# GpSimd in place of VectorE for the lower parts of the first eight weight halves

## The chip, the cores and the metric

The kernel runs on one core of a Trainium2 chip. The metric is device time in microseconds (us), the median of the runs of one launch. Engines are called by the profile's names: PE (TensorE; PEld is its weight load), DVE (VectorE), ACT (ScalarE), POOL (GpSimd), SP (SyncE, which issues transfers here).

## The reference

An attention with a decaying state, a feed-forward layer, and a mixture of eight experts whose weights are balanced by eight rounds of row and column sums:

```python
for t in range(S):                                   # r, k, v, w: (2, 8, 768, 48)
    cur = einsum('bhd,bhe->bhde', u * k_t, v_t)
    y[:, :, t] = einsum('bhd,bhde->bhe', r_t, state + cur)
    state = w_t[..., None] * state + einsum('bhd,bhe->bhde', k_t, v_t)
x = y as (1536, 384)
h = x @ w_in                                         # (384, 2048), float64
x = (h * clip(h + 3, 0, 6) / 6) @ w_out              # (2048, 384), float64
P = exp(x @ w_gate - max); 8 x (rows to 1, columns to N / E)
out = sum over e of P[:, e:e+1] * (max(x @ w1[e], 0) @ w2[e])    # E = 8, F = 1024
```

## The kernel before, in words

Every matmul is made of three in a 32-bit form (`float32r`): each operand is split into an upper part (`hi`, the value rounded to `float32r`) and a lower part (`lo = x - hi`), and the products hi·hi, hi·lo and lo·hi are added in PSUM.

The work has three stages. (1) Attention in 12 steps (six blocks of 128 tokens by two batches), and, woven into it, the feed-forward layer in 96 units. A unit takes 128 of the 2048 hidden columns for 256 tokens: nine matmuls up (`ph`, line 407), ACT adds 3 and clips (`t`, L412), DVE multiplies (L415), ACT takes the upper part `gh` (L419), DVE the lower part `gl` (L423), and nine matmuls down (`xa` and `xb`, L440). (2) From about 298 us on, the eight experts, 24 units each, with 128x512 tiles. (3) The last tiles and their stores.

The feed-forward weights come as float64. They are loaded as 32-bit words in 16 halves, two for each of eight column groups `i`: half `i0` of `w_in` (`n` = 0, tiles `wah` and `wal`) and half `i1` of `w_out` (`n` = 1, tiles `wbh` and `wbl`), 128x768 words after the conversion. `half_steps` gives the steps of one half, which `fast` names by a letter and the two digits:

- `W` (`middle`, L125), `Q` (`top`, L129), `q` (`bottom`, L133): three DVE operations put the float32 bits together in the tile `x`;
- `h` (`upper`, L195): ACT writes the upper part;
- `l` (`lower`, L200): `lo = x - hi`, with both inputs in SBUF.

So `l20` is the lower part of half 0 of group 2. The order of the halves is 00, 01, 10, 11, 20, 21, 30, 31 and so on. The tile `x` has two buffers (`tmp`, `"x"`), so `W` of a half waits until `l` of the half two before it has read its buffer. Expert weights are float32 and need only `h` and `l` (steps `sa` to `se`, later `split_chunk`).

The order of stage 1 is a list of step names, `ORDER`, written out by hand. Each engine takes its instructions in that order, so a step that waits holds up all that stands behind it on its engine. Other steps that the text names, with the chunk's two digits or the unit's number behind: `Z`, `z` (POOL, L280 and L284, 128x384 products) and `D` (DVE, L288, their sums); `N`, `n` (POOL, L320, masks on the attention tile `a`); `Y` (PE, L333 and L337, attention outputs), `y` (DVE, L349, `ys`), `X` (PE, L368, transposes), `H` (ACT, L374, `x1h`), `L` (DVE, L378, `x1l`); `u` (DVE, L358, two updates of the state `st`), `s` (ACT, L363, its decay); `p` and `d` (PE, up and down), `t` (ACT, L412), `g` (DVE, L415), `gh`, `gl` (ACT L419, DVE L423), `oa`, `ob` (the sums of a group of units). `_` is a small matmul that only fills time on PE.

```python
        def lower():
            self.lower_part("ab"[n], q["x"].bitcast(F32), q["hi"], key, eng)
...
    def lower_part(self, nm, x, hi, key, eng):
        lo = self.wp.tile([128, KT * CH], F32R, tag=f"w{nm}l", name=f"w{nm}l")
        eng.tensor_tensor(out=lo, in0=x, in1=hi.bitcast(F32), op=ALU.subtract)
...
    J30 O30 q11 y20 w30 h11 p.4 u20 M21 l11 T21 s20 N21 X20 D21 d.2 t.4 W21 i30 H20 g.4 V21 d.3 L20 Q20 gh.4 p.5 m21
```

The last line is one of the lines of `ORDER`.

Of the kernel before, what the change touches and what calls it, by code (L numbers as in the profile page):

```python
# [94 lines left out]
class Kernel:  # L95
# [803 lines left out]
    def fast(self):  # L899
        tc, nc, pool = self.tc, self.nc, self.pool  # L900
        self.general = False
        with ExitStack() as top:
# [65 lines left out]
            for i in range(F1 // CH):  # L968
                for n in range(2):
                    steps[f"w{i}{n}"] = lambda i=i, n=n: self.load_half(i, n)  # L970
                    for s, fn in zip("WQqhl", self.half_steps(i, n, nc.vector)):
                        steps[f"{s}{i}{n}"] = fn
            for i in range(NCH):
                steps[f"load{i}"] = lambda i=i: self.load_chunk(i)
# [19 lines left out]
            for e in range(1, E):  # L994
                for i in range(NCH):
                    n = (e - 1) * 24 + 4 * i + 6
# [106 lines left out]
```

## Time and profile before

| | before |
|---|---|
| median of 3 runs | 1106.01 us (1104.5 to 1106.65) |
| profiled execution | 1106.59 us, span of its trace 1104.8 us |
| PE busy | 1089.0 us (99%), 6021 matmuls |
| DVE busy | 620.9 us (56%), 1220 instructions |
| ACT busy | 329.7 us (30%), 690 |
| POOL busy | 47.5 us (4%), 54 |
| granted PE clock, mean | 0.990 |

The profile page cuts the span into 40 slices of 27.6 us. Its DVE line begins 8999996: DVE is at 80 to 90% and more of its time through the first six slices (165 us) and near half after that, so the average of 56% hides a first stage in which it has hardly any idle time. A busy PE is not PE at its peak: the granted clock (1.0 is 2.4 GHz, 0.50 is 1.2 GHz) says at what rate it ran. In the timeline, an instruction's start and length are given, and in brackets how long its engine was idle before it and which work ended that.

### The profile page before, as it was taken

What the parts mean: (1) busy time and instruction counts of PE and PEld (TensorE: products, weight loads), DVE (VectorE), ACT (ScalarE), POOL (GpSimd) and SP (SyncE); (2) the same over time, 40 slices, a digit from 0 to 9 for tenths busy, and PEclk for the clock granted to TensorE, in tenths of its full rate; (3) what the DMA queues carried; (4) which work ended last, traced back from release to release, by engine and by line L of the source; (5) the groups of instructions that cost most, each with busy time, mean ns of one, the idle gap of its engine ahead of it and who ended that gap; (6) DMA issues with size and microseconds to landing.
All of it is one profiled execution on the core that took longest, in us unless ns stands there. A gap on an engine that the chain in (4) does not pass through costs nothing.

```text
span 1104.8 us, 14961 instructions
## 1 busy us (share of the span) xinstructions
PE 1089.0 (99%) x6021; PEld 942.9 (85%) x6021; DVE 620.9 (56%) x1220; ACT 329.7 (30%) x690; POOL 47.5 (4%) x54
## 2 busy tenths in 40 slices
PE   9999999999999999999999999999999999999997
PEld 7889999999978888888888888888888888788887
DVE  8999996444533534554564555565466756433231
ACT  4565565544522321221221221122112212221211
POOL 2330042000000000000000000000000000000000
PEclk8899999999999999999999999999999999999999
DMA  8564234000110005013201220313233242100001
GB/s 269 148 184 140 93 102 149 2 1 1 58 58 30 1 6 176 1 42 111 83 26 54 95 78 26 111 56 100 87 114 114 84 144 87 58 1 30 29 15 46
DMA packets 45741, 83.14 MB, mean 75 GB/s; under 512 B 3840, under 2 KB 27744, under 8 KB 45664
## 3 DMA queue, kind: packets, MB, share of 16 engines
q1 hardware_dynamic: 45520, 82.01, 23.3%
q8 instruction: 49, 0.80, 0.3%
q14 instruction: 28, 0.23, 0.1%
q10 hardware_dynamic: 144, 0.10, 0.0%
HBM read 79.69 MB, written 2.41 MB: 74 GB/s over the span
## 4 chain that ended last, share of the span: by engine, by line
PE 91%; DVE 6%; DMA 1%; issue 1%; ACT 1%; SPq 0%; POOL 0%; DVEq 0%; POOLq 0%
PE ph L576 36%; PE y L610 34%; PE ph L407 7%; PE xa L440 5%; PE xb L440 2%; PE y L608 2%; PE y L337 1%; DVE x L133 1%; DVE gl L423 1%; PE sc L304 1%; DVE x L129 1%; DVE t L415 1%; DMA rk<-in_dm_dram 1%; DVE e L238 1%; PE y L333 1%
## 5 line engine op out<-in xcount | busy, mean ns | idle before, releaser
L585 DVE SCALAR_TENSOR_TENSOR hl<-ph,hh 128x512 fp32r<-128x512 f32 x192 | 132.4, 690 | 377.8 <-ACT hh L581 376.7
L581 ACT ACTIVATE hh<-ph 128x512 fp32r<-128x512 f32 x192 | 114.9, 598 | 610.9 <-PE ph L576 610.9
L576 PE MATMUL ph<-x2h,wah 128*128 128x512 f32 x576 | 226.1, 393 | 0.9 <-DVE off L748 0.9
L576 PE MATMUL ph<-x2h,wal 128*128 128x512 f32 x576 | 224.4, 390 | 0.0
L576 PE MATMUL ph<-x2l,wah 128*128 128x512 f32 x576 | 224.2, 389 | 0.0
L610 PE MATMUL y<-hl,wbh 128*128 128x512 f32 x552 | 214.8, 389 | 0.0
L610 PE MATMUL y<-hh,wbh 128*128 128x512 f32 x552 | 214.8, 389 | 0.0
L610 PE MATMUL y<-hh,wbl 128*128 128x512 f32 x552 | 214.7, 389 | 0.0
L576 PEld LDWEIGHTS ph<-x2h,wah 128*128 128x128 f32 x576 | 108.1, 188 | 23.1 <-DVE off L748 1.0
L576 PEld LDWEIGHTS ph<-x2h,wal 128*128 128x128 f32 x576 | 108.1, 188 | 22.9
L576 PEld LDWEIGHTS ph<-x2l,wah 128*128 128x128 f32 x576 | 108.2, 188 | 21.8
L610 PEld LDWEIGHTS y<-hh,wbl 128*128 128x128 f32 x552 | 103.6, 188 | 21.6
L610 PEld LDWEIGHTS y<-hl,wbh 128*128 128x128 f32 x552 | 103.6, 188 | 21.6
L610 PEld LDWEIGHTS y<-hh,wbh 128*128 128x128 f32 x552 | 103.6, 188 | 21.5
L407 PE MATMUL ph<-x1h,wah 128*128 128x256 f32 x288 | 82.6, 287 | 1.0 <-ACT wah L195 1.0
L407 PE MATMUL ph<-x1h,wal 128*128 128x256 f32 x288 | 81.4, 282 | 0.3 <-DVE wal L200 0.3
L407 PE MATMUL ph<-x1l,wah 128*128 128x256 f32 x288 | 81.2, 282 | 0.0
L415 DVE SCALAR_TENSOR_TENSOR t<-t,ph 128x256 f32<-128x256 f32 x96 | 40.0, 418 | 37.1 <-ACT t L412 36.8
L412 ACT ACTIVATE t<-ph,three 128x256 f32<-128x256 f32 x96 | 45.2, 471 | 52.3 <-PE ph L407 51.6
L407 PEld LDWEIGHTS ph<-x1h,wah 128*128 128x128 f32 x288 | 54.7, 190 | 1.9 <-ACT wah L195 1.2
L440 PE MATMUL xa<-gh,wbh 128*128 128x256 f32 x192 | 55.4, 288 | 0.6 <-DVE x2f L452 0.6
L407 PEld LDWEIGHTS ph<-x1h,wal 128*128 128x128 f32 x288 | 54.9, 190 | 0.6 <-DVE wal L200 0.6
(147 smaller groups left out, 1393.2 us busy)
## 6 DMA issues: line engine op xcount, KB each, us to landing
stg<-in_w_dram SPq DMA_DIRECT2D x64, 384.0 KB, 5.1
stg<-in_w_in_dram SPq DMA_DIRECT2D x8, 768.0 KB, 4.9
stg<-in_w_out_dram SPq DMA_DIRECT2D x8, 768.0 KB, 4.4
pb<-pd SPq DMA_DIRECT2D x8, 768.0 KB, 4.2
seen<-in_w_in_dram SPq DMA_DIRECT2D x8, 768.0 KB, 4.9
seen<-in_w_out_dram SPq DMA_DIRECT2D x8, 768.0 KB, 4.4
rk<-in_dm_dram SPq DMA_DIRECT2D x12, 448.0 KB, 4.3
seen<-in_dm_dram SPq DMA_DIRECT2D x12, 448.0 KB, 3.7
```

The costliest lines, as they stand in the source:

```text
L129: nc.vector.scalar_tensor_tensor(out=q["x"], in0=q["high"], scalar=0xC0000000, in1=q["x"], op0=ALU.bitwise_and, op1=ALU.bitwise_or)
L133: nc.vector.scalar_tensor_tensor(out=q["x"], in0=q["low"], scalar=29, in1=q["x"], op0=ALU.logical_shift_right, op1=ALU.bitwise_or)
L238: nc.vector.tensor_tensor_scan(out=e.rearrange("p i t -> p (i t)"), data0=w[:, :WCOL - 1], data1=self.d1e.rearrange("p i t -> p (i t)"), i ...
L407: nc.tensor.matmul(ph, wa[:, kt, :], xa[:, kt, :], start=n == 0, stop=n == 3 * KT - 1)
L412: nc.scalar.activation(q["t"], q["ph"], AF.Relu, bias=self.three)
L415: nc.vector.scalar_tensor_tensor(out=q["t"], in0=q["t"], scalar=6.0, in1=q["ph"], op0=ALU.min, op1=ALU.mult)
L440: nc.tensor.matmul(o, wb[:, kt * 128:(kt + 1) * 128], ga, start=start and n == 0 and kt != 1, stop=stop and n == 2, skip_group_check=True)
L576: nc.tensor.matmul(ph, wa[:, kt, :], xa[:, kt, sl], start=n == 0, stop=n == 3 * KT - 1)
L581: nc.scalar.activation(q["hh"], q["ph"], AF.Relu)
L585: nc.vector.scalar_tensor_tensor(out=hl, in0=q["ph"], scalar=0.0, in1=q["hh"].bitcast(F32), op0=ALU.max, op1=ALU.subtract)
L608: nc.tensor.matmul(y[:, :DM], ha[:, sl], wb, **go)
L610: nc.tensor.matmul(y, wb[:, sl], ha, **go)
```

## The change

In `fast`, the engine handed to the lower part of a half is GpSimd for the groups 0 to 3 (eight halves) and VectorE for the other eight:

```diff
@@ -968,7 +968,7 @@
             for i in range(F1 // CH):
                 for n in range(2):
                     steps[f"w{i}{n}"] = lambda i=i, n=n: self.load_half(i, n)
-                    for s, fn in zip("WQqhl", self.half_steps(i, n, nc.vector)):
+                    for s, fn in zip("WQqhl", self.half_steps(i, n, nc.gpsimd if i < 4 else nc.vector)):
                         steps[f"{s}{i}{n}"] = fn
```

`ORDER` is as it was. The instruction order of PE, ACT and SP is the same; eight instructions leave DVE's list and enter POOL's.

POOL, from the attention of the third chunk on (`wbl` is step `l11`, then `l20`, `l21`, `l30`, `l31`; `rkt` are the steps `Z` and `z`, `a` the masks):

```order
 L280 TENSOR_TENSOR rkt<-rkt 128x384
 L284 TENSOR_TENSOR rkt<-rkt,ubt 128x384
+L200 TENSOR_TENSOR wbl<-x,wbh 128x768
 L320 AFFINE_SELECT a<-a 128x512 x2
 L280 TENSOR_TENSOR rkt<-rkt 128x384
 L284 TENSOR_TENSOR rkt<-rkt,ubt 128x384
+L200 TENSOR_TENSOR wal<-x,wah 128x768
+L200 TENSOR_TENSOR wbl<-x,wbh 128x768
+L200 TENSOR_TENSOR wal<-x,wah 128x768
+L200 TENSOR_TENSOR wbl<-x,wbh 128x768
 L280 TENSOR_TENSOR rkt<-rkt 128x384
```

`l11` now stands ahead of two masks, and `l20` behind the two products of the next chunk.

DVE, around step `l11` (`st_94` is the state update `u20`, the reduction is `D21`, the last row is `W21`):

```order
 L349 TENSOR_TENSOR ys<-y,dv 128x384
 L358 TENSOR_TENSOR st_94<-u,st_94 48x4x48 x2
-L200 TENSOR_TENSOR wbl<-x,wbh 128x768
 L288 TENSOR_REDUCE sd<-rkt 128x8
 L125 TENSOR_SCALAR x<-stg 128x768
```

`W21` needs the buffer that `l11` reads, and `l11` is on another engine now.

DVE, around steps `l20` and `l21` (`ys` is `y21`, `st_95` is `u21`, `x1l` is `L21`, the last row is `W30` and `W31`):

```order
 L349 TENSOR_TENSOR ys<-y,dv 128x384
 L358 TENSOR_TENSOR st_95<-u,st_95 48x4x48 x2
-L200 TENSOR_TENSOR wal<-x,wah 128x768
-L200 TENSOR_TENSOR wbl<-x,wbh 128x768
 L378 TENSOR_TENSOR x1l<-xp,x1h 128x3x128
 L125 TENSOR_SCALAR x<-stg 128x768 x2
```

Two instructions leave the place between the state update `u21` and `L21`. `l30` leaves the place behind the pair `gl.8` and `gl.9`, and `l31` that behind `W40`.

## Rows read from the trace of the kernel before

**Rows 1.** Busy time by engine in three stretches: PE, PEld, DVE, ACT, POOL, PE clock.
```profile
60.00:100.00 40.00, 38.43 (x321) 36.74 (x321) 39.05 (x69) 24.38 (x58) 6.86 (x5) 1.00 0.58 181
100.00:130.00 30.00, 30.00 (x253) 29.70 (x253) 28.70 (x52) 15.30 (x33) 2.36 (x2) 1.00 0.29 95
130.00:165.00 35.00, 33.21 (x311) 31.64 (x309) 34.56 (x63) 21.70 (x63) 11.10 (x12) 1.00 0.32 99
```

**Rows 2.** The chain that ended last, pieces before 100 us: start, us, what.
```profile
36.85 2.01 PE sc L304 x16
...
50.55 6.17 DMA rk<-in_dm_dram
...
82.88 0.86 PE xa L440 x5
```

**Rows 3.** Line 200 on DVE, lower parts of w_out halves: ns min/median/max, first and last start.
```profile
L200 DVE TENSOR_TENSOR wbl<-x,wbh x8: 927/952/959, 37.4 to 140.4; 128x768 fp32r<-128x768 f32 x8
```

**Rows 4.** Timeline of POOL: start, us, what, idle before.
```profile
1.08 0.29 POOL L768 TENSOR_SCALAR_AFFINE_SELECT ident<-ones 128x128 f32<-128x128 f32 x1
...
20.68 1.00 POOL L284 TENSOR_TENSOR rkt<-rkt,ubt 128x384 f32<-128x384 f32 x1
...
44.22 0.64 POOL L320 TENSOR_SCALAR_AFFINE_SELECT a<-a 128x512 f32<-128x512 f32 x1 [3.12 <-ACT a L318]
44.83 1.01 POOL L280 TENSOR_TENSOR rkt<-rkt 128x384 f32<-128x384 f32 x1
...
59.04 3.08 POOL L284 TENSOR_TENSOR rkt<-rkt,ubt 128x384 f32<-128x384 f32 x1
```

**Rows 5.** Timeline of DVE beside two of those POOL products.
```profile
20.71 0.56 DVE L349 TENSOR_TENSOR ys<-y,dv 128x384 f32<-128x384 f32 x1 [1.99 <-PE y L337]
21.18 1.30 DVE L200 TENSOR_TENSOR wal<-x,wah 128x768 fp32r<-128x768 f32 x1
...
44.93 1.18 DVE L423 TENSOR_TENSOR gl<-t,gh 128x256 fp32r<-128x256 f32 x1 [0.34 <-ACT gh L419]
```

**Rows 6.** Timeline of PE where group 1 is first used.
```profile
50.98 0.46 PE L407 MATMUL ph<-x1h,wah 128*128 128x256 f32 x1 [1.03 <-ACT wah L195]
...
51.98 0.58 PE L407 MATMUL ph<-x1h,wal 128*128 128x256 f32 x1 [0.32 <-DVE wal L200]
```

**Rows 7.** Timeline of ACT: steps h11, h20, s21, H21, h30.
```profile
62.97 0.84 ACT L195 ACTIVATE wbh<-x 128x768 fp32r<-128x768 f32 x1 [4.39 <-DVE x L133]
...
70.75 0.83 ACT L195 ACTIVATE wah<-x 128x768 fp32r<-128x768 f32 x1
...
74.93 1.17 ACT L363 ACTIVATE st<-st,pt 112x96 f32<-112x96 f32 x4 [0.66 <-DVE st L358]
76.01 0.47 ACT L374 ACTIVATE x1h<-xp 128x384 fp32r<-128x384 f32 x1
...
80.66 0.84 ACT L195 ACTIVATE wah<-x 128x768 fp32r<-128x768 f32 x1
```

**Rows 8.** Timeline of DVE: steps W21, q21, u21, L21, ob.7, gl.8 with gl.9, W41.
```profile
65.40 0.55 DVE L125 TENSOR_SCALAR x<-stg 128x768 uint32<-128x768 uint32 x1
...
72.45 0.95 DVE L133 SCALAR_TENSOR_TENSOR x<-stg,x 128x768 uint32<-128x768 uint32 x1
...
74.13 0.71 DVE L358 TENSOR_TENSOR st<-u,st 48x192 f32<-48x192 f32 x2
...
76.73 0.56 DVE L378 TENSOR_TENSOR x1l<-xp,x1h 128x384 fp32r<-128x384 f32 x1
...
82.07 0.42 DVE L448 TENSOR_SCALAR x2f<-xb 128x256 f32<-128x256 f32 x1
82.41 0.75 DVE L423 TENSOR_TENSOR gl<-t,gh 128x256 fp32r<-128x256 f32 x2
...
87.34 0.55 DVE L125 TENSOR_SCALAR x<-stg 128x768 uint32<-128x768 uint32 x1
```

**Rows 9.** Busy time and clock in the ten microseconds of group 6.
```profile
50.00:60.00 10.00, 8.70 (x63) 8.41 (x64) 9.36 (x18) 7.04 (x21) 3.56 (x4) 0.83 0.68 207
```

## The prediction

> **What bounds the kernel now.** I read the busy times by stretch first. From 60 to 100 us DVE is busy for 39.05 of 40 us and PE stands idle for 1.57; from 100 to 130 us PE has no idle time; from 130 to 165 us it is idle for 1.79 again [rows 1]. The reader is to see two things: PE is the bound of the whole, DVE is nearly level with it before 165 us, and a microsecond that PE loses before 100 us can't be made up, since PE is full behind it. In the other direction there is little to win: all PE idle time in the DVE-bound stretch is 1.57 us.
>
> Next the chain that ended last. Before 45 us it runs over PE (scores at 36.85), at 50.55 over a 6.17 us transfer of `rk`, from there over DVE, and at 82.88 it goes to PE for good, behind `gl.8` [rows 2]. So lateness of DVE between 56 and 83 us counts, and what happens to DVE before 50 us is covered by PE and that transfer.
>
> Last the timelines, for what a GpSimd product does to its neighbours [rows 4, 5]. This is the main point.
>
> **The price of a lower part on GpSimd.** On DVE it takes 0.95 us [rows 3]. No 128x768 operation on POOL is in the trace. From below I bound it by DVE's 0.95, from above by twice a 128x384 product, 2 x 1.01 = 2.0. A select takes 0.29 for 128 columns and 0.64 for 512, which leaves 0.17 fixed; (1.01 - 0.17) x 2 + 0.17 = 1.85 us, which I take [rows 4].
>
> The GPSIMD Engine Reference of the Trainium skill (section 3.1) gives 4497 ns for a two-input operation of 2048 columns; an estimate from that page for 768 columns is 1.69 us, and with it each of the three waits below would be 0.16 shorter, the sum 2.1 in place of 2.55. The row differs, 1.01 for 384 columns where that rate gives an estimate of 0.84, so the row decides.
>
> **What it does to DVE meanwhile.** Two `gl` take 0.75 together at 82.41 and one takes 1.18 at 44.93; the difference of 0.8 lies beside the POOL product at 44.83. At 20.68 another product starts: `ys`, which reads PSUM and one SBUF tile, takes 0.56, and the lower part behind it 1.30 in place of 0.95, since the product is not over before 21.68 [rows 3 to 5, 8]. So a DVE operation with two SBUF inputs waits for most of a POOL product, some 0.8 of 1.01 us, and one with a PSUM input doesn't. For a lower part I take 1.65 of its 1.85 us (bounds: 0 and 2.0).
>
> SBUF — State Buffer of the Trainium skill (section Who interferes with whom) says that such a DVE operation and a GpSimd operation that reads SBUF exclude each other for the whole instruction, and that the one issued first blocks the other. The traced blocks are a little shorter than the whole; by that page's rule two terms below would each be 0.2 larger, and the sum 2.95.
>
> **The change, term by term,** in times of the old trace.
>
> `l00`, `l01`, `l10`: 0. The first two lie where PE leads [rows 2]. `l10` comes 1 us later to PE, which waited 0.32 for it at 51.98 [rows 6]; DVE then waits for the `rk` transfer, which was issued behind `q10`, ahead of `l10`. If that cover is gone, the price is 1.0.
>
> `l11`: `W21` needs the buffer of `x` that `l11` reads. `h11` ends at 62.97 + 0.84 = 63.81, GpSimd needs 1.85 more, with 0.1 for two handovers 65.8; `W21` was at 65.40 [rows 7, 8]. **+0.4.** From below: 0.95 gives 64.9, no loss. From above: the mask queued behind `l11` on POOL holds `W21` for another 0.5. The 0.95 us that left DVE win nothing, since `W21` is next but one.
>
> `l20`: `h20` ends at 71.58; ACT is 0.4 to 0.5 late there, the products ahead on POOL are done, and GpSimd begins near 72.1 and blocks until 73.8. `q21`, two SBUF inputs, was due at 72.45 + 0.4 = 72.85 [rows 7, 8]. **+1.0** (0 to 1.3).
>
> The gap of `l20` and `l21`: `L21` needs `x1h`, and so `u21`, then `s21` and `H21` on ACT. Before, `u21` ended at 74.84 and `L21` began at 76.73, 1.89 later; the two lower parts filled that gap. Without them it is 0.09 to start ACT, 1.08 and 0.47 of work and a handover, 1.7: **-0.2** and not the 1.7 us that left DVE [rows 7, 8]. `l21` runs on GpSimd meanwhile and blocks nobody.
>
> `l30`: `h30` (80.66 to 81.5) is 1.2 late by now, so `l30` is ready at 82.7. `Q31`, two inputs from SBUF, keeps it out until `ob.7`, one from PSUM, which began at 82.07 and is due at 83.3; there GpSimd gets in and holds until 84.95. `gl.8` was due at 82.41 + 1.2 = 83.6 [rows 7, 8]. **+1.35** (0 to 1.6). PE waits for `gl.8` at 82.88 [rows 2], so the lateness passes to PE here.
>
> `l31`: `W41`, before at 87.34, waits for it as `W21` did for `l11` [rows 8]; but PE, itself 2.5 late by then, feeds the DVE rows around it, and that lateness covers the wait. 0.
>
> Sum: 0.4 + 1.0 - 0.2 + 1.35 = **2.55 us** (bounds -0.2 and 3.8, from the ends named). Behind 100 us nothing gives it back [rows 1]. The weight loads that the `q` steps release go later by no more than this, and the order of SP is unchanged. The profiled execution took 1106.59, 0.58 above the median; against the median, 1106.01 + 2.55, some **1108.6 us**.
>
> **The rivals.**
>
> *No blocking.* GpSimd takes 1.85 us but DVE runs on. For it: the DVE operations with a PSUM input do so, and a POOL product took 3.08 at 59.04, so POOL can also be the one that waits [rows 4, 5]. Against it: 0.8 us lost where a product met a two-input operation. Then only the waits stay: `W21` +0.4, the gap -0.2, `gl.8` +0.2, and 1106.2 us. It decides if `q21` and `gl.8` keep their lengths and starts. This is the case that ends on the other side, no slower than before.
>
> *PE falls to the lower clock.* PE stood for 1.03 us at 50.98, and behind it a matmul takes 0.46 and 0.58; the mean granted clock of these 10 us is 0.83, so it was at 0.50 (1.2 GHz) for 3.4 of them [rows 6, 9]. The forecast has new waits of a microsecond or more: at 51.98, before the transposes that need `y21`, and before `gl.8`. That spell cost 1.7 us of work. One or two between 73 and 90 us add 1.5 to 3: 1110.1 to 1111.6. Against it: from 60 to 100 us PE stood for 1.57 in all and the clock stayed at 1.00 [rows 1].
>
> *DVE gains.* The lower parts end on GpSimd before anyone needs them and DVE gets the room. Its most is PE's idle time: 1.57 us, 1104.4; only with the stretch behind 130 us as well, 3.36 in all, 1102.7 [rows 1]. It needs a lower part on GpSimd near 1 us.
>
> **How the numbers follow.** About 0.2%, 2.2 us, can be told from no change here. Forecast 0.60: its sum lies near that bound, 0.43 of it above and 0.17 below. No blocking 0.22, all within. Lower clock 0.12, all slower. DVE gains 0.06, of which 0.05 faster, 0.01 within. So faster 0.05, same 0.40, slower 0.55. The range begins at 1105.0, no blocking with an execution's scatter, and ends at 1111.8, the dear end of the lower clock; left out are most of the gains and the tails, under 0.2.
>
> **What would show it.** Eight rows of line 200 on POOL with a shortest length near 1.85. `q21` starting about a microsecond behind its neighbour `g.6`, or drawn out to 1.9; `gl.8` drawn out by over a microsecond; `W21` with an idle time ahead of it that ends with POOL; `L21` as late behind `u21` as before, with DVE idle between. PE's wait before `gl.8` longer, PE from 100 to 130 us still without idle time, and the clock at 1.00 from 60 us on. It is wrong if `gl.8` starts within 0.5 us of 82.41, if POOL's rows of line 200 are near 1 us, or if the difference arises behind 100 us.

## The result and the profile after

| | before | changed |
|---|---|---|
| median of 6 runs each, us | 1104.61 (1103.28 to 1106.65) | 1110.92 (1108.73 to 1113.14) |
| ratio, 95% interval | 1 | 1.0061 [1.0046, 1.0075] |
| profiled execution, its span, us | 1106.59, 1104.8 | 1113.14, 1111.4 |

The change makes the kernel slower by 6.7 us (5.1 to 8.3) by the ratio; the medians lie 6.3 apart. The direction and the range of the prediction held. The size did not: the sum gave 2.55 us. Part of the closeness of 1108.6 to 1110.92 is luck, since before came out 1.4 us lower in six runs than in the first three. That the range held is luck of the same kind: seen from 1106.01, the median it was built on, it reached from -1.0 to +5.8 us, and the measured loss lies above that.

The profiled execution of the changed kernel is the slowest of its six. It is already 1.3 us late when PE starts on group 1 (`52.28`, before 50.98 [rows 6]). That much is scatter between executions or an effect of the early pieces; the experiments come back to it.

First the page of the changed kernel: the span, and busy time, share and instructions of each engine.

```profile
span 1111.4 us, 14960 instructions
...
PE 1089.3 (98%) x6021; PEld 943.2 (85%) x6021; DVE 617.3 (56%) x1212; ACT 330.0 (30%) x690; POOL 61.4 (6%) x62
```

Next line 200 in it, grouped by engine: ns min/median/max, first and last start; below that, who waited for these instructions (us, times).

```profile
L200 POOL TENSOR_TENSOR wal<-x,wah x4: 1810/1999/2519, 21.1 to 86.9; 128x768 fp32r<-128x768 f32 x4
L200 POOL TENSOR_TENSOR wbl<-x,wbh x4: 1822/1842/1997, 39.4 to 92.2; 128x768 fp32r<-128x768 f32 x4
...
  DVE x L125: 2.7, 3
```

Eight products run on POOL, the shortest in 1.81 us (forecast 1.85, on DVE 0.95 [rows 3]). Three times the next step `W` on DVE stands behind one of them.

Then the stretches of the changed kernel, columns as in [rows 1].

```profile
60.00:100.00 40.00, 35.41 (x289) 34.21 (x288) 33.28 (x57) 21.83 (x54) 15.37 (x10) 0.96 0.48 148
100.00:130.00 30.00, 30.00 (x256) 29.89 (x255) 28.55 (x51) 15.20 (x33) 2.24 (x2) 1.00 0.43 138
...
70.00:80.00 10.00, 7.59 (x63) 7.39 (x62) 8.76 (x12) 5.53 (x16) 7.46 (x5) 0.94 0.69 227
80.00:90.00 10.00, 8.63 (x63) 8.26 (x63) 7.94 (x14) 4.56 (x11) 2.18 (x1) 0.89 0.29 92
```

From 60 to 100 us DVE falls from 39.05 to 33.28 us busy, with 57 instructions in place of 69: some went to POOL, others now come later than 100 us. Yet PE's idle time there grows from 1.57 to 4.59. From 100 to 130 us PE has no idle time, as before: nothing is given back. New is the granted clock: 0.94 and 0.89 in the two stretches where it was 1.00 before.

The timeline of DVE in the changed kernel shows the steps of [rows 8]: `W21`, `q21`, `gl.6`, `u21`, `L21`, `gl.8` with `gl.9`, `W41` (start, us, what, idle before and what ended it).

```profile
66.97 0.97 DVE L125 TENSOR_SCALAR x<-stg 128x768 uint32<-128x768 uint32 x1 [1.13 <-POOL wbl L200]
...
74.30 1.42 DVE L133 SCALAR_TENSOR_TENSOR x<-stg,x 128x768 uint32<-128x768 uint32 x1
75.64 2.03 DVE L423 TENSOR_TENSOR gl<-t,gh 128x256 fp32r<-128x256 f32 x1
...
78.06 0.71 DVE L358 TENSOR_TENSOR st<-u,st 48x192 f32<-48x192 f32 x2
80.45 0.56 DVE L378 TENSOR_TENSOR x1l<-xp,x1h 128x384 fp32r<-128x384 f32 x1 [1.67 <-ACT x1h L374]
...
87.66 2.04 DVE L423 TENSOR_TENSOR gl<-t,gh 128x256 fp32r<-128x256 f32 x2
...
94.08 0.56 DVE L125 TENSOR_SCALAR x<-stg 128x768 uint32<-128x768 uint32 x1 [0.32 <-POOL wbl L200]
```

And POOL beside them in the same execution: `l11`, `l20`, `l21`, `l30`.

```profile
65.11 1.82 POOL L200 TENSOR_TENSOR wbl<-x,wbh 128x768 fp32r<-128x768 f32 x1 [4.24 <-ACT wbh L195]
...
74.87 2.52 POOL L200 TENSOR_TENSOR wal<-x,wah 128x768 fp32r<-128x768 f32 x1
77.35 2.00 POOL L200 TENSOR_TENSOR wbl<-x,wbh 128x768 fp32r<-128x768 f32 x1
86.89 2.18 POOL L200 TENSOR_TENSOR wal<-x,wah 128x768 fp32r<-128x768 f32 x1 [7.55 <-ACT wah L195]
```

For `gl.6` and for PE's first step behind `y21`, these are the rows of the kernel before:

```profile
73.32 0.41 DVE L423 TENSOR_TENSOR gl<-t,gh 128x256 fp32r<-128x256 f32 x1
...
74.26 0.55 PE L368 MATMUL xp<-ident,ys 128*128 128x128 f32 x3 [0.38 <-DVE ys L349]
```

Read DVE and POOL together. `gl.6`, a product of 256 columns, takes 2.03 us while `l20` runs (0.41 before); the pair `gl.8`, `gl.9` takes 2.04 while `l30` runs (0.75 before). `W21` stands 1.13 us for `l11`. `L21` begins 1.68 us after `u21` ends, with DVE idle: the gap that the lower parts had filled (1.89 before).

What it does to PE, in PE's timeline of the changed kernel.

```profile
54.17 0.38 PE L407 MATMUL ph<-x1h,wal 128*128 128x256 f32 x1 [1.39 <-POOL wal L200]
...
78.19 0.55 PE L368 MATMUL xp<-ident,ys 128*128 128x128 f32 x3 [2.41 <-DVE ys L349]
...
89.41 0.39 PE L440 MATMUL xa<-gl,wbh 128*128 128x256 f32 x1 [1.37 <-DVE gl L423]
```

PE's waits at these three places are 1.4 to 2.4 us long; before they were 0.32 [rows 6], 0.38 (the row above) and none. Behind the second its matmuls run at the lower clock for a while. The chain of the changed kernel that ended last shows it (start, us, what):

```profile
65.11 1.83 POOL wbl L200
...
75.72 1.95 DVE gl L423
...
80.55 1.85 PE ph L407 x9
```

Nine matmuls of `ph` take 1.85 us; in the repeat of this kernel below, with the clock at 1.00, nine take 1.06. POOL, which is busy for 6% of the span, now stands on the chain.

### The profile page after: what moved, and what is told of

Read it like the earlier page. It is cut to its first block, busy times and chain, and to the rows that moved or that the text cites. A ratio compares the mean times of both kernels' runs of the same rounds, so it can differ in the third digit from the quotient of the medians.

```text
span 1111.4 us, 14960 instructions
## 1 busy us (share of the span) xinstructions
PE 1089.3 (98%) x6021; PEld 943.2 (85%) x6021; DVE 617.3 (56%) x1212; ACT 330.0 (30%) x690; POOL 61.4 (6%) x62
## 3 DMA queue, kind: packets, MB, share of 16 engines
HBM read 79.69 MB, written 2.41 MB: 74 GB/s over the span
## 4 chain that ended last, share of the span: by engine, by line
PE 90%; DVE 6%; ACT 1%; issue 1%; DMA 1%; POOL 0%; SPq 0%; DVEq 0%; ACTq 0%; POOLq 0%
PE ph L576 35%; PE y L610 34%; PE ph L407 8%; PE xa L440 5%; PE xb L440 3%; PE y L608 2%; PE y L337 1%; DVE gl L423 1%; DVE x L133 1%; DVE x L129 1%; DVE e L238 1%; DVE f L248 1%; DMA w<-in_dm_dram 1%; DVE t L415 1%; PE sc L304 0%
## 5 line engine op out<-in xcount | busy, mean ns | idle before, releaser
L423 DVE TENSOR_TENSOR gl<-t,gh 128x256 fp32r<-128x256 f32 x96 | 46.0, 481 | 20.5 <-ACT gh L419 19.4
L440 PE MATMUL xa<-gl,wbh 128*128 128x256 f32 x192 | 54.4, 284 | 2.4 <-DVE gl L423 2.4
```

The source lines that it names most:

```text
L423: nc.vector.tensor_tensor(out=gl, in0=q["t"], in1=q["gh"].bitcast(F32), op=ALU.subtract)
L440: nc.tensor.matmul(o, wb[:, kt * 128:(kt + 1) * 128], ga, start=start and n == 0 and kt != 1, stop=stop and n == 2, skip_group_check=True)
```

## The experiments

The theories: **blocking** (a product that reads SBUF on GpSimd holds DVE operations with two SBUF inputs), **waits** (`W` and PE stand for lower parts that come later), **clock** (PE's new waits lower the granted clock), and **DVE's room** (the time that left DVE could be worth something if GpSimd cost nothing). Where a placement is changed, `(i, n)` is the half, and `l20` that of half (2, 0). Times are medians; ratios are to before in the same comparison, whose medians were 1103.70 to 1103.96 us. A ratio, with its 95% interval, is not that of the two medians; a loss in us is worked out from the ratio.

### Three early lower parts alone

```
- self.half_steps(i, n, nc.gpsimd if i < 4 else nc.vector)
+ self.half_steps(i, n, nc.gpsimd if (i, n) in ((0, 0), (0, 1), (1, 0)) else nc.vector)
```

> Only l00, l01 and l10 go to GpSimd, the other five lower parts of the first eight stay on DVE. Theory A (the cost lies where DVE is on the chain, 56 to 98 us, by blocked two-input operations and waits for x): within 1 us of the kernel before; PE's wait for l10 grows by about 1.1 us and is covered. Theory B (the first blame belongs to PE's wait for l10 and the low clock behind it): 1.5 to 3 us slower than before.

1104.30 us (1103.35 to 1108.76, 12 runs), ratio 1.0018 [1.0003, 1.0033]: 2.0 us, between 0.3 and 3.6. The medians lie only 0.3 apart; four of the twelve runs stand above 1107 and make the rest. This decides for neither theory: the interval reaches from under 1 us to over 3.

### The other five alone

The same line with `((1, 1), (2, 0), (2, 1), (3, 0), (3, 1))`.

> Only l11, l20, l21, l30 and l31 go to GpSimd. Theory A: nearly all of the loss of the change stays, 4 to 6 us slower than before, with gl.6 and the pair gl.8 and gl.9 drawn out by 1.3 us or more. Theory B: less than half of it stays, under 3 us.

1107.30 us (1105.56 to 1109.21, 12 runs), ratio 1.0034 [1.0023, 1.0045]: 3.8 us, between 2.5 and 5.0. The timelines of DVE (first two rows, `gl.6` and `gl.8` with `gl.9`) and POOL (`l20`) in this kernel:

```profile
71.50 2.03 DVE L423 TENSOR_TENSOR gl<-t,gh 128x256 fp32r<-128x256 f32 x1
...
81.99 2.04 DVE L423 TENSOR_TENSOR gl<-t,gh 128x256 fp32r<-128x256 f32 x2
...
70.65 2.60 POOL L200 TENSOR_TENSOR wal<-x,wah 128x768 fp32r<-128x768 f32 x1 [1.43 <-ACT wah L195]
```

The same blocks at the same places, with the clock at 1.00 from 50 us on. So the five late pieces cost most of the loss, and they do it without the clock. The loss is a little under the 4 to 6 us that were expected of them.

### Writes in place of reads

In the eight places the lower part is left out (PE reads the upper part in its stead) and GpSimd clears `x` twice, which reads nothing from SBUF.

```
  def lower_part(...):
+     if eng is self.nc.gpsimd:
+         eng.memset(x, 0.0)
+         eng.memset(x, 0.0)
+         self.wt[key] = hi, hi
+         return
```

> The eight lower parts are left out (PE reads the upper part in their place); where each stood, GpSimd clears the x tile twice, which writes 128x768 two times and reads nothing. W of the half after next still waits for GpSimd. Theory A, blocking by GpSimd's reads: two-input DVE operations keep their lengths beside these writes; only the waits for x are left, the time is within 1.5 us of before, on either side. Theory C, any work of GpSimd holds DVE up: 3 to 6 us slower, with gl drawn out as in the changed kernel.

1104.53 us (1101.51 to 1106.76, 12 runs), ratio 1.0006 [0.9993, 1.0019]. DVE and POOL in this kernel, around the places of `l20` and `l30` (lines of the kernel stand 5 lower in the file here, so L428 is `gl`):

```profile
74.03 0.41 DVE L428 TENSOR_TENSOR gl<-t,gh 128x256 fp32r<-128x256 f32 x1
...
82.90 0.75 DVE L428 TENSOR_TENSOR gl<-t,gh 128x256 fp32r<-128x256 f32 x2
...
73.96 0.74 POOL L201 MEMSET x<- 128x768 f32 x1
...
82.92 0.74 POOL L201 MEMSET x<- 128x768 f32 x1
```

`gl.6` and `gl.8` keep the lengths they had before, 0.41 and 0.75, though POOL works beside them for 0.74 us. So it is the reads on GpSimd that hold DVE, not that POOL is busy. The lengths show this, the time less so: PE, which takes the upper part, does not wait for the clears, so its waits for lower parts are gone here too. SBUF — State Buffer of the Trainium skill (section Who interferes with whom) says so in its rule that a DVE instruction with two SBUF inputs contends with a GpSimd instruction that reads SBUF and not with one that only writes it; the trace agrees, with 0.41 against 2.03 us.

### The eight lower parts left out, nothing in their place

```
+     if eng is self.nc.gpsimd:
+         self.wt[key] = hi, hi
+         return
```

> The eight lower parts are left out on every engine (PE reads the upper part in their place). This is the most that freeing DVE of them can bring. Theory A (the lower parts mostly filled gaps, and PE's idle time there is 1.6 us): 0 to 1.6 us faster than before. Theory D (DVE's 7.6 us were worth having, and GpSimd's cost ate them): 3 us faster or more.

1104.20 us (1099.78 to 1108.54, 12 runs), ratio 1.0008 [0.9994, 1.0023]. PE reads the upper part where the lower one was, as above. Even with these eight operations gone altogether, some 7.6 us of DVE's work, no gain can be measured; one over 0.7 us lies outside the interval. (The clock may hide about one more: see the table further below, where this kernel stands 2 us above before.) That is little of the 7.6 us, so DVE's room is settled: most of the operations filled gaps in which DVE waits for ACT or PE, and taking them off DVE pays next to nothing, whoever does them.

### The changed kernel again

No edit; it stands in the comparison of the next two.

> The changed kernel once more, on the chip and against the runs of the kernel before of this comparison. If its parts add, it is early3 plus late5: 0.18% + 0.34%, 5 to 7 us slower than before. If more than 8 us, something acts only when both sets are on GpSimd.

1110.38 us (1108.57 to 1112.88, 6 runs), ratio 1.0060 [1.0038, 1.0081]: 6.6 us. The 2.0 of the early three and the 3.8 of the late five make 5.8, so within the intervals the two sets add. Its profiled execution took 1109.61 us and has the clock at 1.00 from 60 us on, so here the steps can be read without the clock. PE starts on group 1 at 50.54, 0.4 us ahead of before, so the 1.3 us by which the first profile was late there need not come with the change. DVE's timeline (`W21`, `q21`, `L21`, `gl.8`) and the stretches of 70 to 90 us of this run:

```profile
65.57 0.97 DVE L125 TENSOR_SCALAR x<-stg 128x768 uint32<-128x768 uint32 x1 [1.13 <-POOL wbl L200]
...
73.44 2.26 DVE L133 SCALAR_TENSOR_TENSOR x<-stg,x 128x768 uint32<-128x768 uint32 x1
...
78.81 0.56 DVE L378 TENSOR_TENSOR x1l<-xp,x1h 128x384 fp32r<-128x384 f32 x1 [1.68 <-ACT x1h L374]
...
84.50 2.04 DVE L423 TENSOR_TENSOR gl<-t,gh 128x256 fp32r<-128x256 f32 x2
```

```profile
70.00:80.00 10.00, 7.83 (x69) 7.62 (x69) 8.31 (x13) 5.07 (x13) 6.41 (x4) 1.00 0.69 215
80.00:90.00 10.00, 8.63 (x71) 8.26 (x70) 8.63 (x15) 5.26 (x11) 3.14 (x2) 1.00 0.35 100
```

`l20` holds `q21` here (2.26 us in place of 0.95 [rows 8]) and leaves `gl.6` alone; in the first profile it was mostly the other way round. Which of the two meets the read varies, the loss hardly.

### The early three taken apart

The same line with `((0, 0), (0, 1))`, and with `((1, 0),)`.

> Only l00 and l01 go to GpSimd. Theory E (the loss of early3 is theirs: the masks behind l00 reach PE late, and W10 waits for l01): 1 to 2.5 us slower than before. Theory F (it is l10's): within 0.8 us of before. The forecast had 0 for both.

> Only l10 goes to GpSimd. Theory F (PE stands about 1.1 us longer before the third matmul of p.2, and its clock falls or stays low more often behind that): 1 to 2.5 us slower than before, with executions at the lower clock from 51 us on. Theory E: within 0.8 us of before.

1105.60 us, ratio 1.0006 [0.9993, 1.0020]; and 1103.88 us, 1.0002 [0.9989, 1.0016], 12 runs each. Neither is measurable alone by its ratio, though the median of the first lies 1.9 us above that of before. The sum of the two ratios, 0.9 us, and the 2.0 of the three together agree within the intervals, so whether the early three cost one microsecond or two is not settled.

### Two pieces that block, three that make others wait

The same line with `((2, 0), (3, 0))`, and with `((1, 1), (2, 1), (3, 1))`.

> Only l20 and l30 go to GpSimd, the two whose reads meet two-input operations of DVE (q21 or gl.6, and the pair gl.8 and gl.9). If blocking is the main cost: 2 to 3.5 us slower than before, with 1.3 to 1.7 us more on gl.6 or q21 and 1.3 more on the pair. If the waits are the main cost: under 1 us.

> Only l11, l21 and l31 go to GpSimd, those for which DVE waits (W21, W41) or which fall into the gap before L21. If blocking is the main cost: within 1.2 us of before; the forecast has +0.4 for l11 and 0 for the other two. If the waits are: 2 us slower or more.

The two that block: 1106.92 us (10 runs), ratio 1.0023 [1.0013, 1.0033], 2.5 us. Forecast for these two terms: 1.0 + 1.35 = 2.35. Its profiled execution, the slowest of its ten with 1111.07, has the lower clock in the same place as the first profile of the changed kernel:

```profile
70.00:80.00 10.00, 7.67 (x56) 7.46 (x56) 9.27 (x13) 4.36 (x11) 4.79 (x3) 0.85 0.72 222
80.00:90.00 10.00, 8.63 (x70) 8.26 (x69) 8.38 (x15) 5.17 (x11) 2.18 (x1) 0.98 0.26 82
```

The three that make others wait: 1105.87 us (12 runs), ratio 1.0021 [1.0010, 1.0031], 2.3 us, a good deal over the 0.2 that the sum gave them (+0.4, -0.2 and 0). By what was expected ahead of the run, 2 us or more speaks for the waits. DVE's timeline in this kernel shows part of the reason:

```profile
62.59 0.97 DVE L125 TENSOR_SCALAR x<-stg 128x768 uint32<-128x768 uint32 x1 [1.13 <-POOL wbl L200]
...
72.82 2.15 DVE L200 TENSOR_TENSOR wal<-x,wah 128x768 fp32r<-128x768 f32 x1
```

`W21` waits 1.13 us and is then itself drawn out from 0.55 to 0.97, beside the mask that had queued up on POOL behind `l11`. And this split has a block of its own: `l20`, back on DVE, runs beside `l21` on GpSimd and takes 2.15 us in place of 0.96. Together with what else shifts, `L21` begins 15.3 us after `y20` (59.70 to 75.00) where it was 13.9 before (62.86 to 76.73), so 1.4 of the 2.3 us are seen here, in the fastest of the twelve executions. So the pieces don't add up singly; what stands beside them changes with each split.

### A buffer of its own for the `x` of half 11

Four buffers for the tile `x` in place of two would spare every such wait, but they do not fit: the pool `att` needs 48.6 KB of SBUF per partition, and 45.8 would be left. So here, in the changed kernel, only half 11 gets a buffer of its own, and `W21` need not wait for `l11`:

```
- q["x"] = self.tmp.tile([128, KT * CH], U32, tag="x", name="x")
+ q["x"] = (self.att if (i, n) == (1, 1) and not self.general else self.tmp).tile(...)
```

> The changed kernel with a buffer of its own for x of half 11, so that W21 needn't wait for l11 (nor l11 hold it up but by its reads). Theory G (the wait is a cost of its own): 0.8 to 1.2 us faster than all8, W21 at once behind D21. Theory H (the reads of l11 hold W21 there instead): no faster than all8 by more than 0.4 us, W21 drawn out to 1.5 us or more.

1108.88 us (1106.99 to 1112.01, 6 runs), ratio 1.0054 [1.0037, 1.0071]: 0.6 us less than the changed kernel's 6.6, well within the intervals. DVE and POOL at this place:

```profile
63.67 1.63 DVE L125 TENSOR_SCALAR x<-stg 128x768 uint32<-128x768 uint32 x1
...
63.03 1.85 POOL L200 TENSOR_TENSOR wbl<-x,wbh 128x768 fp32r<-128x768 f32 x1 [4.80 <-ACT wbh L195]
```

The wait is gone and the block has taken its place: `W21`, with one SBUF input, is drawn out to 1.63 us and ends after the product on GpSimd has ended. So in this trace `l11` holds `W21` with the shared buffer or without it; the times alone cannot tell the two apart.

### Work for PE in its longest new wait

Small matmuls of no use to the result, ahead of the transposes that need `y21`, in the changed kernel: first 24 into the buffer of the transposes, then 20 into a free one.

```
+ if (c, b) == (2, 1):
+     fp = self.psg.tile([128, 512], F32, tag="g", name="fp")
+     for _ in range(20):
+         nc.tensor.matmul(fp[:, :256], self.warm[:, :128], self.warm, start=True, stop=True)
```

> The changed kernel with 24 small matmuls on PE ahead of the transposes X21, into the tile that these then write, so that PE works through its longest new wait. Theory K (idle PE loses its clock behind 76 us in some executions, and this is part of the loss): the granted clock stays at 1.00 from 70 to 90 us, 0.5 to 1.5 us faster than all8. Theory L (DVE alone sets the end): no change, or up to 0.5 us slower.

> In fill_x21 the small matmuls stood behind the wait for y21, since their tile was the one that ys had to free, and not inside it. Here 20 of them go into a free buffer of ph, so that PE works while it waits. Theory K (idle PE loses its clock behind 76 us in some executions, and this is part of the loss): clock 1.00 from 70 to 90 us, 0.5 to 1.5 us faster than all8, so 0.45% to 0.55% slower than before. Theory L (DVE alone sets the end): 0.6% slower as all8.

The first missed: 1111.71 us, ratio 1.0074 [1.0056, 1.0092]. Its matmuls stood behind the wait instead of in it, as PE's timeline shows, and only lengthened the way:

```profile
75.30 4.45 PE L369 MATMUL xp<-warm 128*128 128x256 bf16 x24 [2.40 <-DVE ys L349]
```

The second fills the wait: 1108.78 us (1106.31 to 1109.57, 8 runs), ratio 1.0039 [1.0026, 1.0053], 4.3 us. PE's timeline, and the stretches from 70 to 90 us:

```profile
73.17 2.36 PE L369 MATMUL fp<-warm 128*128 128x256 bf16 x20
```

```profile
70.00:80.00 10.00, 9.90 (x87) 9.37 (x87) 8.31 (x13) 4.67 (x12) 5.73 (x4) 1.00 0.70 221
80.00:90.00 10.00, 8.63 (x71) 8.25 (x70) 8.12 (x14) 5.45 (x12) 4.04 (x2) 1.00 0.39 116
```

DVE is held as in the changed kernel: `q21` takes 2.25 us and `gl.8` with `gl.9` 2.04. Yet it takes some 2 us less than the 6.6 beside it, and the dearest of its runs is 1109.57 where the changed kernel's are 1112.88 and 1113.14.

The two intervals still overlap a little, so here is a second reading of the same runs. Each has its span and its mean granted clock; span x (1 - clock) is the work that the lower clock kept from PE, idle stretches included.

| kernel | runs | mean of span x (1 - clock), us |
|---|---|---|
| before, all comparisons with the experiments | 92 | 6.1 |
| changed, first runs | 6 | 10.0 |
| changed, repeat | 6 | 11.5 |
| changed, own buffer for half 11 | 6 | 10.9 |
| changed, small matmuls behind the wait | 6 | 9.8 |
| the five late ones | 12 | 5.2 |
| the three early ones | 12 | 7.3 |
| the eight left out | 12 | 8.1 |
| writes in place of reads | 12 | 7.1 |
| changed, PE's wait filled | 8 | 6.0 |

The four kernels not shown in it, with one to three of the eight on GpSimd, stand at 5.5 to 6.9. All four readings of the eight together stand some 4 to 5 us above before, and with one wait of PE filled it is at before's level. A difference of 2 shows nothing here: the kernel with the eight left out has it, and loses no time that can be measured. Among the runs of before, a microsecond more in this sum goes with 0.4 to 0.55 us more time, so 4 to 5 of it answer to about 2 us: what filling the wait took off. That is an estimate, since in the profile of before the clock was lowered ahead of 60 us (0.83 on average) and stood at 1.00 behind, and what it costs behind 76 us may differ.

## Why the prediction was right, and where it was too small

**Right: the bound and what follows from it.** PE is full behind 100 us, so what is lost before stays lost. `sc` that starts at 148.23 us before starts at 154.77 after, 6.5 later, and the end is 6.6 later. The row of before and that of the first profile of the changed kernel:

```profile
148.23 1.16 PE L304 MATMUL sc<-rk 48*128 48x128 f32 x16 [0.62 <-DVE rk L257]
...
154.77 1.16 PE L304 MATMUL sc<-rk 48*128 48x128 f32 x16 [0.62 <-DVE rk L257]
```

And DVE's room is worth next to nothing: this rested on PE's 1.57 us of idle time [rows 1] and is shown, to about a microsecond, by the kernel without the eight operations.

**Right: the price and the block.** A lower part takes 1.81 us against the 1.85 worked out from a product of 384 and two selects [rows 4]. That DVE operations with two SBUF inputs stand still for most of it was the main point; the rows of 2.03 to 2.26 show it, some 1.3 to 1.6 us longer than before where 1.65 was taken, and the clears on GpSimd show that it is the reads.

**The terms, by the repeat of the changed kernel,** whose clock is at 1.00 in this stretch as it was before. Lateness is taken against the old trace, from the end of `q11` (62.93 before, 62.76 in the repeat). Rows of DVE that the table and the text below it use, `q11` and `Q21` before, then the same two in the repeat, and last the mask on POOL behind `l11` in the repeat:

```profile
61.28 1.65 DVE L133 SCALAR_TENSOR_TENSOR x<-stg,x 128x768 uint32<-128x768 uint32 x1
...
69.97 1.10 DVE L129 SCALAR_TENSOR_TENSOR x<-stg,x 128x768 uint32<-128x768 uint32 x1
...
61.80 0.96 DVE L133 SCALAR_TENSOR_TENSOR x<-stg,x 128x768 uint32<-128x768 uint32 x1
...
70.54 1.51 DVE L129 SCALAR_TENSOR_TENSOR x<-stg,x 128x768 uint32<-128x768 uint32 x1
...
65.48 0.64 POOL L320 TENSOR_SCALAR_AFFINE_SELECT a<-a 128x512 f32<-128x512 f32 x1
```

| term | forecast, us | measured, us | by |
|---|---|---|---|
| `l11` | +0.4 | +0.76 | `W21` ends 65.95 before, 66.54 now |
| `l20` | +1.0 | +1.7 | `q21` ends 73.40 before, 75.70 now |
| gap of `l20` and `l21` | -0.2 | -0.2 | `L21` starts 76.73 before, 78.81 now |
| `l30` | +1.35 | +1.3 | `gl.9` ends 83.16 before, 86.54 now |
| sum | 2.55 | 3.55 | |

So two terms were too small. **`l11`**: the wait itself was about as forecast, 0.34 of the 0.76. The other 0.42 is `W21` drawn out to 0.97 beside the mask behind `l11`; the text had this as its bound from above (another 0.5) and did not take it. **`l20`**: the block on `q21` alone is 1.31 us, the forecast's upper end; the 0.4 beside it is the `Q` ahead of it, 1.10 us before and 1.51 now; POOL's product of `rkt` comes at another time against it, which is argued and not tested. The rest holds: `l30` within 0.1, the gap to the tenth; `l31` makes `W41` wait 0.32 us, which PE's lateness covers; and the early ones can't be measured singly. The forecast's upper bound, 3.8, comes out of the ends that it names only without the -0.2 of the gap (3.6 with it), and without the 1.0 named for `l10`.

The 3.55 us agree with what the five late pieces cost alone (3.8, 2.5 to 5.0), and with the changed kernel whose PE wait is filled (4.3).

**The step that fell short** beside these two terms is the sum's silence on the clock. The forecast set "PE falls to the lower clock" beside itself as a rival with 0.12, on the ground that the clock had stayed at 1.00 from 60 to 100 us with 1.57 us of idle time. But the forecast's own waits make more: PE stands 2.2 to 2.4 us before it can transpose `y21` (0.38 before), and 1.37 for `gl.8`. In the first profile the clock is at 0.94 and 0.89 there, in the repeat at 1.00. So it falls in some executions, and one sign that the forecast named, the clock at 1.00 from 60 us on, failed in the first profile. What it cost in that execution can be read: from the start of `L21` to the end of `gl.9` it takes 9.25 us (80.45 to 89.70), the repeat 7.73 (78.81 to 86.54), 1.5 less with the same 2.04 us for the pair. Over the runs it makes up some 2 of the 6.7 us, an estimate from the kernel with PE's wait filled. The rival was not an alternative to the sum but a further term of it, and its time, 1110.1 to 1111.6, is where the measurement lies, helped by a start that was 1.4 us too high. The 3.55 us and these 2 leave about 1 of the 6.7 without a cause, inside the interval.

**Open:** where the clock that the eight together lose lies. Behind PE's wait for `y21` the profiles show at most one spell, 1.7 us in the sum of the table, in the first profile and in that of the two that block; the 4 to 5 us of the table are more. In the profile with a buffer of its own for half 11 the clock is low from 50 to 60 us (0.66) and at 1.00 behind, PE waits only 0.23 us for `y21`, and the sum of this execution is still 9.9. And the five late ones, with a wait of 2.23 us before `y21`'s transposes, do not lose it (5.2). So it is shown over the runs that the sum falls when the wait is filled; how the two hang together is not. Whether the early three cost one microsecond or two is open as well. With 2.0 for them and 3.8 for the late five the loss is nearly added up without a term for the clock, so part of the 2 us put down to the clock may be theirs.

## What to carry to other kernels

An operation that fills a gap in which its engine would wait anyway costs little or nothing there, and moving it off wins as little: ask first what a kernel without it would take. On GpSimd its cost is less its length than what stands beside it: here DVE operations with two SBUF inputs that met the product were held for some 1.2 to 1.6 us, and so, by 1.1, was the wide one-input `W` once. And where a forecast holds new waits of PE, the clock behind them belongs into the sum, not only among the rivals.

## What the runs showed of the hardware that was not expected

- A DVE operation with one SBUF input can be held too: `W` (128x768, 0.55 us alone) took 1.63 beside a product on GpSimd. The forecast's sum counted on two-input operations only; just its upper bound for `l11` let a mask on POOL hold `W` for 0.5.
- How far it goes the other way: a product on GpSimd takes 1.81 us at the shortest, and 2.5 to 2.6 where a two-input operation of DVE is already under way.
- The granted clock behind nearly the same wait of PE differs between executions of one kernel: 0.94 and 0.89 behind 2.41 us in one, 1.00 behind 2.17 in the other.
